# Sigmoid attention and a SwiGLU block on one core: attention in 64x64 tiles of the array, q and k turned by DMA, engine orders written by hand

## The chip, the core and the metric

The kernel runs on one core of one Trainium2 chip. TensorE (PE in the profile, PEld for its weight loads) multiplies, ScalarE (ACT) takes sigmoids, VectorE (DVE) and GpSimd (POOL) copy and cast, and the DMA engines move data; SyncE (SP) and POOL issue the DMAs. The metric is the device time of one run in microseconds (us); lower is better. A program and its data do not change from run to run.

## The reference

```python
B, H, S, D = 8, 12, 448, 64          # q, k, v: float32
scores = q @ k.T / sqrt(D) - log(S)  # for each batch and head
attn   = sigmoid(scores) @ v         # 448 x 64 for each head
x      = attn, heads side by side    # 3584 tokens x 768
g, val = x @ w_gate, x @ w_val       # 768 -> 1536
out    = (g * sigmoid(g) * val) @ w_out   # 1536 -> 768, float32
```

The sigmoid acts on each score by itself, so no sum over a row is needed before the product with v.

## The kernel before, in words

Tokens are cut into chunks of 112 (448 = 4 x 112). For each batch, `emit_load` (L101) brings q, k and v in twelve DMAs of 112 tokens x 12 heads x 64 (pieces of 256 bytes), and `emit_cast` (L109) makes bfloat16 or float16 of them, on GpSimd from the second batch on. `emit_tr` (L121) turns q and k on TensorE, two heads at a time, into tiles of 128 x 448 (rows 0 to 63 hold one head, 64 to 127 the next) through one PSUM buffer, and DVE copies them to SBUF (L132).

For each head, `emit_qk` (L142) makes four score tiles of 112 keys x 448 queries: 64 rows of the array contract, so half of it is used. `emit_sig` takes the sigmoid on ACT (L163). `emit_pv` (L165) multiplies by v: four matmuls with 112 rows and 64 columns. DVE casts the 64 x 448 result into one half of a tile xT (L185), which holds x transposed, 128 features x 448 tokens.

The feed-forward part (FFN) of a batch takes 12 steps f. In each, `emit_ffn1_mm` (L190) runs six matmuls for the gate and six for the value, 128 x 128 weights against 128 x 448 tokens; ACT takes the sigmoid (L205), and DVE makes t (L207) and hT (L209). `emit_ffn2` (L215) makes the output in units of 112 tokens x 384 columns, twelve matmuls each, into the PSUM buffer that the transposes use as well; ACT writes the unit to osb (L230) and POOL issues the store (L235).

A loop over g and j writes attention of batch g, the first FFN part of batch g-1 and the second of batch g-2 into one another, and the framework's scheduler sets the final order of each engine from that. Weights come in 36 DMAs on SP, three for each j, and are cast on ACT and DVE (L88, L90).

PSUM has eight banks: "A" 4 (scores), "P" 1 (pv), "G" 2 (gate, value), "TO" 1:

```python
ps = psum.tile([128, S], BF16, tag="TO", bufs=1, name="ps_tr")
pv = psum.tile([D, S], FP32, tag="P", bufs=1, name="ps_pv")
o = psum.tile([PC, 384], FP32, tag="TO", bufs=1, name="ps_o")
```

Of the kernel before, what the change touches and what calls it, by code (L numbers as in the profile page):

```python
# [12 lines left out]
COPY = mybir.ActivationFunctionType.Copy  # L13
# [5 lines left out]
def kernel(  # L19
# [10 lines left out]
    nc = tc.nc  # L30

# [3 lines left out]
    PC = 112  # L35
    NC_ = S // PC
    NP = H // 2
    NF = DFF // 128
    HSC = 4096.0
# [5 lines left out]
    psum = ctx.enter_context(tc.tile_pool(name="ps", bufs=1, space=bass.MemoryType.PSUM))  # L45
    stg = ctx.enter_context(tc.tile_pool(name="stg", bufs=1))
    one = ctx.enter_context(tc.tile_pool(name="one", bufs=1))
    two = ctx.enter_context(tc.tile_pool(name="two", bufs=2))
    wp = ctx.enter_context(tc.tile_pool(name="wp", bufs=1))
    attn = ctx.enter_context(tc.tile_pool(name="attn", bufs=4))  # L50
    ptp = ctx.enter_context(tc.tile_pool(name="ptp", bufs=8))
    xtp = ctx.enter_context(tc.tile_pool(name="xtp", bufs=12))
    htp = ctx.enter_context(tc.tile_pool(name="htp", bufs=22))
    osp = ctx.enter_context(tc.tile_pool(name="osp", bufs=2))

    idn = one.tile([PC, PC], BF16, tag="idn")
    make_identity(nc, idn)
    sb_t = one.tile([128, 1], FP32, tag="sbiast")
    nc.gpsimd.memset(sb_t, sbias)

    wg16 = [wp.tile([128, DFF], FP16, tag=f"wg{j}", name=f"wg16_{j}") for j in range(NP)]
    wv16 = [wp.tile([128, DFF], FP16, tag=f"wv{j}", name=f"wv16_{j}") for j in range(NP)]
    wo16 = [wp.tile([128, DM], FP16, tag=f"wo{f}", name=f"wo16_{f}") for f in range(NF)]

    wjobs = []
    for j in range(NP):
        rows = slice(j * 128, (j + 1) * 128)
        for h2 in range(2):
            cols = slice(h2 * DM, (h2 + 1) * DM)
            wjobs.append((moe_w_gate[rows, cols], wg16[j][:, cols]))  # L70
            wjobs.append((moe_w_val[rows, cols], wv16[j][:, cols]))
    for f in range(NF):
        rows = slice(f * 128, (f + 1) * 128)
        wjobs.append((moe_w_out[rows, :], wo16[f][:, :]))
    NWJ = len(wjobs)
    wstage = {}

    def emit_wload(i):
        src, _ = wjobs[i]
        st = stg.tile([128, DM], FP32, tag="wst", bufs=4, name=f"wst{i}")  # L80
        nc.sync.dma_start(out=st, in_=src)
        wstage[i] = st

    def emit_wcast(i, eng=None):
        _, dst = wjobs[i]
        eng = eng or nc.scalar
        if eng is nc.scalar:
            eng.copy(out=dst, in_=wstage.pop(i))  # L88
        else:
            eng.tensor_copy(out=dst, in_=wstage.pop(i))  # L90

    q16 = {}
# [24 lines left out]

    qTt = {}
    kTt = {}

    def emit_tr(b, p, which):  # L121
        src = (q16, k16)[which][b]
        ps = psum.tile([128, S], BF16, tag="TO", bufs=1, name="ps_tr")
        for c in range(NC_):
            nc.tensor.transpose(  # L125
                out=ps[:, c * PC:(c + 1) * PC],
                in_=src[:, c, 2 * p:2 * p + 2, :],
                identity=idn,
            )
        d, nm = ((qTt, "qT"), (kTt, "kT"))[which]  # L130
        t = attn.tile([128, S], BF16, tag=nm, name=f"{nm}_{b}_{p}")
        nc.vector.tensor_copy(out=t, in_=ps)  # L132
        d[(b, p)] = t

    def emit_tr_sched(g, j):
        if j < 8:
            btr, ptr = g, j // 2 + 2
        else:
            btr, ptr = g + 1, (j - 8) // 2
        if btr < B and ptr < NP:  # L140
            emit_tr(btr, ptr, j % 2)

    def emit_qk(b, h, cs):
        p, which = divmod(h, 2)
        ro = which * D
        qT = qTt[(b, p)]
        kT = kTt[(b, p)]
        outs = []
        for c in cs:
            sc = psum.tile([PC, S], FP32, tag="A", bufs=4, name="ps_sc")  # L150
            nc.tensor.matmul(  # L151
                out=sc,
                lhsT=kT[ro:ro + D, c * PC:(c + 1) * PC],
                rhs=qT[ro:ro + D, :],
                start=True,
                stop=True,
            )
            pt = ptp.tile([PC, S], FP16, tag="pt", name="pt")
            outs.append((sc, pt))
        return outs  # L160

    def emit_sig(sc, pt):
        nc.scalar.activation(out=pt, in_=sc, func=SIGM, bias=sb_t[:PC], scale=qkscale)  # L163

    def emit_pv(b, h, pts):  # L165
        pv = psum.tile([D, S], FP32, tag="P", bufs=1, name="ps_pv")
        for c in range(NC_):
            nc.tensor.matmul(  # L168
                out=pv,
                lhsT=v16[b][:, c, h, :],  # L170
                rhs=pts[c],
                start=(c == 0),
                stop=(c == NC_ - 1),
            )
        return pv

    xT = {}
    hT = {}

    def emit_pvcast(b, h, pv):  # L180
        p, which = divmod(h, 2)
        ro = which * D
        if which == 0:
            xT[(b, p)] = xtp.tile([128, S], FP16, tag="xT", name=f"xT_{b}_{p}")
        nc.vector.tensor_copy(out=xT[(b, p)][ro:ro + D, :], in_=pv[0:D, :])  # L185

    pvq = []

    def emit_ffn1_mm(b, f, gate):
        ps = psum.tile([128, S], FP32, tag="G", bufs=2,  # L190
                       name="ps_g" if gate else "ps_vl")
        w = wg16 if gate else wv16
        for j in range(NP):
            nc.tensor.matmul(  # L194
                out=ps,
                lhsT=w[j][:, f * 128:(f + 1) * 128],
                rhs=xT[(b, j)],
                start=(j == 0),
                stop=(j == NP - 1),
            )  # L200
        return ps

    def emit_ffn1_post(b, f, gps, vps):
# [6 lines left out]
            out=ht, in0=vps, scalar=HSC, in1=t1, op0=MULT, op1=MULT  # L210
        )
        hT[(b, f)] = ht

    osb_cur = [None]

    def emit_ffn2(b, u):
# [141 lines left out]
```

## Time and profile before

| what | value |
|---|---|
| three runs | 645.62, 647.29, 647.56 us; median 647.29 |
| span of the profiled execution | 646.1 us |
| PE, PEld busy | 610.1 us (94%), 297.3 us (46%) |
| ACT, DVE, POOL busy | 321.8 us (50%), 220.9 us (34%), 85.9 us (13%) |
| moved | 58.71 MB, 91 GB/s over the span |

The page gives no device time for the profiled execution other than its span. The span runs from the first to the last instruction; the runs' times also hold what lies around it. An engine's busy time is the union of its instructions. PE's matmuls overlap in the pipeline, so a row of several matmuls lasts longer than the engine needs before the next may start; starts of rows that follow each other tell the pace.

### The profile page before, as it was taken

The page shows a single profiled execution, that of the slowest core. Times are in us where ns is not written, and L with a number is a line of the kernel's source. Part 1 is how long each engine was busy: PE and PEld are TensorE (multiplying, and loading weights), DVE is VectorE, ACT ScalarE, POOL GpSimd, SP SyncE. Part 2 cuts the span into 40 slices and gives each one's busy share as a digit, 9 for nine tenths or more (in the row PEclk, how much of TensorE's full clock was granted, in tenths as well). Part 3 has the DMA queues.
Part 4 walks back from the last instruction along what each step waited for, and adds up shares of the span by engine and source line. Part 5 has one row for each costly group of instructions (what it writes and reads, how often), then busy time and mean ns, then how long its engine had stood idle before and what let it go on. Part 6 is the DMA issues. An engine that isn't in the chain of part 4 may idle for free.

```text
span 646.1 us, 7821 instructions
## 1 busy us (share of the span) xinstructions
PE 610.1 (94%) x3072; PEld 297.3 (46%) x3072; DVE 220.9 (34%) x402; ACT 321.8 (50%) x576; POOL 85.9 (13%) x123
## 2 busy tenths in 40 slices
PE   0899879999999999999999999999999999999985
PEld 0332323344555455444555455544545454546653
DVE  0232326444333432344333433344333433333310
ACT  4767537655545554455445554555445544542221
POOL 0011110351231102210040102110000000000000
PEclk9999999999999999999999999999999999999999
DMA  9956986995695423704092400010010000000112
GB/s 191 203 144 164 231 243 186 208 208 106 137 218 117 102 50 78 136 23 85 22 173 62 87 23 21 22 30 14 22 43 22 1 23 21 22 22 22 44 43 65
DMA packets 138341, 58.71 MB, mean 91 GB/s; under 512 B 131648, under 2 KB 131648, under 8 KB 138304
## 3 DMA queue, kind: packets, MB, share of 16 engines
q1 hardware_dynamic: 135744, 47.19, 35.3%
q0 software_dynamic: 2560, 11.01, 5.5%
q8 instruction: 24, 0.39, 0.3%
q14 instruction: 13, 0.11, 0.1%
HBM read 47.19 MB, written 11.01 MB: 90 GB/s over the span
## 4 chain that ended last, share of the span: by engine, by line
PE 60%; issue 32%; POOL 2%; ACT 2%; SPq 1%; DMA 1%; DVE 1%; POOLq 0%; ACTq 0%
PE ps_sc L151 12%; PE ps_g L194 12%; PE ps_pv L168 12%; PE ps_vl L194 11%; PE ps_o L223 10%; PE ps_tr L125 4%; SPq L106 1%; POOL out_dram L235 1%; DMA kst<-in_k_dram 1%; ACT pt L163 1%; POOL v L116 0%; DVE xT L185 0%; DVE kT L132 0%; ACT wg L88 0%; ACT L163 0%
## 5 line engine op out<-in xcount | busy, mean ns | idle before, releaser
L163 ACT ACTIVATE pt<-ps_sc,sb_t 112x448 f16<-112x448 f32 x384 | 222.4, 636 | 102.2 <-PE ps_sc L151 93.0
L223 PE MATMUL ps_o<-wo,hT 128*112 128x384 f16 x768 | 135.7, 326 | 4.2 <-ACT osb L230 4.2
L194 PE MATMUL ps_g<-xT,wg 128*128 128x448 f16 x576 | 131.7, 361 | 2.2 <-DVE t L207 1.3
L194 PE MATMUL ps_vl<-xT,wv 128*128 128x448 f16 x576 | 129.3, 359 | 0.3 <-DVE t L207 0.3
L151 PE MATMUL ps_sc<-qT,kT 64*112 64x448 bf16 x384 | 121.9, 409 | 2.9 <-ACT pt L163 2.8
L223 PEld LDWEIGHTS <-hT 128*112 128x112 f16 x768 | 99.8, 130 | 35.4 <-issue 5.6
L168 PE MATMUL ps_pv<-pt,v 112*64 112x448 f16 x384 | 110.2, 390 | 1.6 <-ACT pt L163 1.2
L207 DVE TENSOR_TENSOR t<-ps_g,s 128x448 f16<-128x448 f32 x96 | 60.0, 625 | 149.0 <-ACT s L205 148.8
L205 ACT ACTIVATE s<-ps_g 128x448 f16<-128x448 f32 x96 | 52.2, 544 | 91.1 <-PE ps_g L194 89.5
L230 ACT ACTIVATE osb<-ps_o 112x384 f32<-112x384 f32 x64 | 31.4, 491 | 113.5 <-PE ps_o L223 113.5
L194 PEld LDWEIGHTS <-wg 128*128 128x128 f16 x576 | 50.0, 99 | 72.3 <-issue 35.5
L194 PEld LDWEIGHTS <-wv 128*128 128x128 f16 x576 | 50.0, 98 | 68.2 <-issue 31.2
L185 DVE CAST xT<-ps_pv 64x448 f16<-64x448 f32 x96 | 59.3, 617 | 61.0 <-PE ps_pv L168 60.3
L209 DVE SCALAR_TENSOR_TENSOR hT<-ps_vl,t 128x448 f16<-128x448 f32 x96 | 60.0, 625 | 46.7 <-PE ps_vl L194 44.6
L235 POOL DMA_DIRECT2D out_dram<-osb x32 | 17.0, 531 | 364.6 <-ACT osb L230 364.6
L151 PEld LDWEIGHTS <-kT 64*112 64x112 bf16 x384 | 35.8, 133 | 59.3 <-issue 56.9
L168 PEld LDWEIGHTS <-v 112*64 112x64 f16 x384 | 36.4, 114 | 54.1 <-issue 36.5
L132 DVE COPY qT<-ps_tr 128x448 bf16<-128x448 bf16 x48 | 18.7, 389 | 76.2 <-PE ps_tr L125 76.2
L132 DVE COPY kT<-ps_tr 128x448 bf16<-128x448 bf16 x48 | 18.7, 389 | 64.2 <-PE ps_tr L125 64.2
L125 PE MATMUL ps_tr<-idn,q 112*128 112x112 bf16 x192 | 21.6, 233 | 16.4 <-ACT q L114 14.5
L116 POOL CAST q<-qst 112x768 bf16<-112x768 f32 x28 | 22.6, 830 | 86.6 <-DMA qst<-in_q_dram 62.6
L116 POOL CAST v<-vst 112x768 f16<-112x768 f32 x28 | 22.9, 843 | 79.6 <-DMA vst<-in_v_dram 40.6
(20 smaller groups left out, 107.7 us busy)
## 6 DMA issues: line engine op xcount, KB each, us to landing
qst<-in_q_dram SPq DMA_DIRECT2D x32, 336.0 KB, 5.9
kst<-in_k_dram SPq DMA_DIRECT2D x32, 336.0 KB, 6.2
vst<-in_v_dram SPq DMA_DIRECT2D x32, 336.0 KB, 5.6
out_dram<-osb POOLq DMA_DIRECT2D x32, 336.0 KB, 3.0
wst<-in_moe_w_gate_dram SPq DMA_DIRECT2D x12, 384.0 KB, 4.2
wst<-in_moe_w_val_dram SPq DMA_DIRECT2D x12, 384.0 KB, 4.5
wst<-in_moe_w_out_dram SPq DMA_DIRECT2D x12, 384.0 KB, 3.8
```

The lines of the kernel that those rows point to most:

```text
L116: eng.tensor_copy(out=t[:, c], in_=st)
L125: nc.tensor.transpose(out=ps[:, c * PC:(c + 1) * PC], in_=src[:, c, 2 * p:2 * p + 2, :], identity=idn,)
L132: nc.vector.tensor_copy(out=t, in_=ps)
L151: nc.tensor.matmul(out=sc, lhsT=kT[ro:ro + D, c * PC:(c + 1) * PC], rhs=qT[ro:ro + D, :], start=True, stop=True,)
L163: nc.scalar.activation(out=pt, in_=sc, func=SIGM, bias=sb_t[:PC], scale=qkscale)
L168: nc.tensor.matmul(out=pv, lhsT=v16[b][:, c, h, :], rhs=pts[c], start=(c == 0), stop=(c == NC_ - 1),)
L185: nc.vector.tensor_copy(out=xT[(b, p)][ro:ro + D, :], in_=pv[0:D, :])
L194: nc.tensor.matmul(out=ps, lhsT=w[j][:, f * 128:(f + 1) * 128], rhs=xT[(b, j)], start=(j == 0), stop=(j == NP - 1),)
L205: nc.scalar.activation(out=s16, in_=gps, func=SIGM)
L207: nc.vector.tensor_tensor(out=t1, in0=gps, in1=s16, op=MULT)
L209: nc.vector.scalar_tensor_tensor(out=ht, in0=vps, scalar=HSC, in1=t1, op0=MULT, op1=MULT)
L223: nc.tensor.matmul(out=o, lhsT=hT[(b, f)][:, tci * PC:(tci + 1) * PC], rhs=wo16[f][:, half * 384:(half + 1) * 384], start=(f == 0), stop=( ...
```

## The change

The whole body is written anew. Its parts:

- Four heads make a group; there are 24 groups (three for each batch). Heads 2j and 2j+1 lie on partitions 0 to 63 and heads 6+2j and 7+2j on 64 to 127. Tokens are taken as (p c) with c = 7, so a DMA piece is 1,792 bytes (`load`, two DMAs of 64 partitions for each of q, k and v).
- `cast` makes 128 x 896 tiles. For the first three groups `trans_pe` turns q and k on TensorE (42 matmuls in all); for the other 21 groups `trans_dma` has SP issue a DMA transpose from SBUF to SBUF, 42 in all.
- `qk_tile` makes 64 keys x 448 queries of four heads with four matmuls, each in a quarter of the array of 64 rows x 64 columns; `pv` does the same for the product with v. There are 168 tiles, so 672 matmuls of each kind. One sigmoid covers 128 x 896 elements.
- The FFN's first part stays (1,152 matmuls); the second works on 128 tokens across two batches: 28 chunks x 2 halves x 12 matmuls = 672 of them, evicted on DVE.
- `manual_schedule` leaves each engine's order as the code writes it: FFN units one after another, and between them "visits" of two score tiles of the next batch, with `pv` of a finished group.
- PSUM: two score buffers of two banks, and four banks "G" for all else. Weights come in 18 DMAs of 768 KB through three buffers; gate and value are cast on DVE, w_out on POOL.

Cut to its core:

```diff
-    psum = ctx.enter_context(tc.tile_pool(name="ps", bufs=1, space=bass.MemoryType.PSUM))
+    ctx.enter_context(tc.manual_schedule())
+    psA = ctx.enter_context(tc.tile_pool(name="psA", bufs=2, space=bass.MemoryType.PSUM))
+    psG = ctx.enter_context(tc.tile_pool(name="psG", bufs=4, space=bass.MemoryType.PSUM))
...
+    def load(n, which):
+        b, j = divmod(n, NJ)
+        src = (q, k, v)[which]
+        st = stg.tile([128, 2, S], FP32, tag="stg", name=f"st{which}_{n}")
+        for w in range(2):
+            h0 = w * (H // 2) + 2 * j
+            nc.sync.dma_start(
+                out=st[w * 64:(w + 1) * 64],
+                in_=src[b, h0:h0 + 2].rearrange("h (p c) d -> p h (c d)", c=C),
+            )
...
+    def trans_dma(n, which):
+        t = q16.pop((n, which))
+        d = qkT.tile([128, C, 128], BF16, tag=f"T{which}", name=f"T{which}_{n}")
+        nc.sync.dma_start_transpose(out=d, in_=t.rearrange("p c h d -> p (c h d)"))
+        qT[(n, which)] = d
...
+    def qk_tile(n, c):
+        sc = psA.tile([128, 2, 512], FP32, tag="A", name="ps_sc")
+        qt, kt = qT[(n, 0)], qT[(n, 1)]
+        for w in range(2):
+            for h2 in range(2):
+                r = slice(h2 * 64, h2 * 64 + 64)
+                nc.tensor.matmul(
+                    out=sc[w * 64:(w + 1) * 64, h2, :S],
+                    lhsT=kt[r, c, w * 64:(w + 1) * 64],
+                    rhs=qt[r, :, w * 64:(w + 1) * 64],
+                    start=True,
+                    stop=True,
+                )
+        return sc
+
+    def sig_tile(n, c, sc):
+        pt = ptp.tile([128, 2, S], FP16, tag="pt", name="pt")
+        nc.scalar.activation(out=pt, in_=sc[:, :, :S], func=SIGM, bias=sb_t, scale=qkscale)
+        pts[(n, c)] = pt
+
+    def pv(n):
+        b, j = divmod(n, NJ)
+        P = [psG.tile([128, S], FP32, tag="G", name=f"ps_pv{w}") for w in range(2)]
+        vt = v16.pop(n)
+        for c in range(C):
+            pt = pts.pop((n, c))
+            for h2 in range(2):
+                for w in range(2):
+                    r = slice(w * 64, w * 64 + 64)
+                    nc.tensor.matmul(
+                        out=P[w][h2 * 64:(h2 + 1) * 64, :],
+                        lhsT=vt[r, h2, c * D:(c + 1) * D],
+                        rhs=pt[r, h2, :],
+                        start=(c == 0),
+                        stop=(c == C - 1),
+                    )
+        for w in range(2):
+            x = xtp.tile([128, S], FP16, tag="xT", name=f"xT_{b}_{w * NJ + j}")
+            nc.vector.tensor_copy(out=x, in_=P[w])
...
+    def ffn2(b, m, half):
...
+        o = psG.tile([128, hw], FP32, tag="G", name="ps_o")
+        for f in range(NF):
+            h = hT[(b // 2, f)].rearrange("p b s -> p (b s)")
+            lhsT = h[:, m * 128:(m + 1) * 128]
...
+        nc.vector.tensor_scalar(
+            out=osb[:, half * hw:(half + 1) * hw], in0=o, scalar1=HREC, scalar2=None, op0=MULT
+        )
...
+    for dur, u in units:
+        while vi < len(visits) and tcur >= vtime[vi]:
+            group = visits[vi]
+            vi += 1
+            pvs, pend = pend, []
+            attn_step(group, pvs)
...
+                        if casted <= nn:
+                            cast(nn, 0, nc.gpsimd)
+                            cast(nn, 1, nc.gpsimd)
+                            trans_dma(nn, 0)
+                            trans_dma(nn, 1)
+                            cast(nn, 2, nc.gpsimd)
...
+        while wcq and ui >= 1.5 * wk:
+            kind, i = wcq.pop(0)
+            w_cast(kind, i, nc.gpsimd if kind == "o" else nc.vector)
+            if wl:
+                w_load(*wl.pop(0))
+            wk += 1
```

`attn_step` runs `qk_tile` for the two tiles of a visit, then `pv` of a group that is finished, then the two sigmoids.

The order on ACT in the middle of the run, which follows the matmuls on PE: pt is a score tile's sigmoid, s a gate's, osb an output unit.

```order
L205 ACTIVATE s_1532<-ps_g 128x448
L163 ACTIVATE pt<-ps_sc,sb_t 112x448 x3
L230 ACTIVATE osb_0_1470<-ps_o 112x384
L163 ACTIVATE pt<-ps_sc,sb_t 112x448
L205 ACTIVATE s_1603<-ps_g 128x448
```

```order
L159 ACTIVATE pt<-ps_sc,sb_t 128x896 x2
L199 ACTIVATE s_1414<-ps_g 128x448
L199 ACTIVATE s_1433<-ps_g 128x448
L159 ACTIVATE pt<-ps_sc,sb_t 128x896 x2
L199 ACTIVATE s_1466<-ps_g 128x448
```

The first fence is the kernel before, four narrow sigmoids for each gate with an output unit among them; the second is the change, two wide ones for one or two gates, and the output unit has left ACT.

The order on DVE where the first batch's FFN begins: t and hT free a gate's and a value's PSUM bank, wg and wv are weights, and wst is the buffer that their DMA fills.

```order
L90 CAST wv_4_102<-wst_390 128x768
L90 CAST wv_4_102<-wst_430 128x768
L207 TENSOR_TENSOR t_715<-ps_g,s_713 128x448
L90 CAST wv_5_103<-wst_469 128x768
L207 TENSOR_TENSOR t_769<-ps_g,s_767 128x448
L209 SCALAR_TENSOR_TENSOR hT_0_717<-ps_vl,t_715 128x448
```

```order
L180 CAST xT_5_519<-ps_pv_488 128x448
L201 TENSOR_TENSOR t_577<-ps_g,s_575 128x448
L87 CAST wg_2_105<-wst_g_467 128x1536
L206 SCALAR_TENSOR_TENSOR hT_0_589<-ps_vl,t_577 128x448
L87 CAST wv_2_111<-wst_v_469 128x1536
L201 TENSOR_TENSOR t_617<-ps_g,s_615 128x448
L87 CAST wg_3_106<-wst_g_471 128x1536
L206 SCALAR_TENSOR_TENSOR hT_1_629<-ps_vl,t_617 128x448
```

Before, nearly all value weights are cast ahead of the first t; in the change a third of the gate and value weights are, and the other casts stand between the t and hT of the first FFN steps.

The order on SP in the change at the same place; T_5 are the turned q and k of group 5, c_0 and c_1 their casts on POOL, st the loads.

```order
L81 DMA wst_v_669<-in_moe_w_val_dram 128x6x256
L81 DMA wst_o_692<-in_moe_w_out_dram 128x2x768
L99 DMA st_6_742<-in_q_dram 64x2x448 x2
L99 DMA st_6_745<-in_k_dram 64x2x448 x2
L99 DMA st_6_748<-in_v_dram 64x2x448 x2
L124 DMA_TRANSPOSE T_5_755<-c_0_5_751 128x7x128
L124 DMA_TRANSPOSE T_5_757<-c_1_5_753 128x7x128
L81 DMA wst_o_773<-in_moe_w_out_dram 128x2x768
```

The transposes stand in the same queue as all loads; the rest of w_out comes behind the loads of group 6 and the transposes of group 5.

## Rows read from the trace of the kernel before

**Rows 1.** The page: the span, and part 1, busy time by engine.

```profile
span 646.1 us, 7821 instructions
...
PE 610.1 (94%) x3072; PEld 297.3 (46%) x3072; DVE 220.9 (34%) x402; ACT 321.8 (50%) x576; POOL 85.9 (13%) x123
```

**Rows 2.** Busy time by stage: stretch, length, engines (instructions), granted clock, DMA share, GB/s.

```profile
20.00:60.00 40.00, 37.06 (x115) 12.95 (x114) 11.04 (x22) 28.48 (x49) 5.18 (x6) 1.00 0.65 159
60.00:100.00 40.00, 33.04 (x110) 11.91 (x110) 12.48 (x26) 18.91 (x31) 5.33 (x6) 1.00 0.88 229
...
300.00:400.00 100.00, 100.00 (x533) 50.20 (x532) 35.56 (x65) 50.59 (x95) 15.77 (x22) 1.00 0.29 63
400.00:500.00 100.00, 100.00 (x535) 50.21 (x533) 35.68 (x65) 50.54 (x94) 9.51 (x14) 1.00 0.09 25
```

**Rows 3.** PE in order of time from 303.9 us: start, length, row, count.

```profile
304.00 0.58 PE L151 MATMUL ps_sc<-qT,kT 64*112 64x448 bf16 x2
304.51 1.31 PE L194 MATMUL ps_g<-xT,wg 128*128 128x448 f16 x6
305.75 0.58 PE L151 MATMUL ps_sc<-qT,kT 64*112 64x448 bf16 x2
306.27 1.31 PE L194 MATMUL ps_vl<-xT,wv 128*128 128x448 f16 x6
307.41 2.11 PE L223 MATMUL ps_o<-wo,hT 128*112 128x384 f16 x12
309.46 0.38 PE L168 MATMUL ps_pv<-pt,v 112*64 112x448 f16 x1
```

**Rows 4.** PE in order of time, 18 to 36 us.

```profile
26.78 0.62 PE L151 MATMUL ps_sc<-qT,kT 64*112 64x448 bf16 x1
...
34.32 0.62 PE L151 MATMUL ps_sc<-qT,kT 64*112 64x448 bf16 x2
```

**Rows 5.** Groups by line: count, busy us, mean ns of one, idle before.

```profile
L163 ACT ACTIVATE pt<-ps_sc,sb_t 112x448 f16<-112x448 f32 x384 | 222.4, 636 | 102.2 <-PE ps_sc L151 93.0 <-PE ps_pv L168 8.7
...
L209 DVE SCALAR_TENSOR_TENSOR hT<-ps_vl,t 128x448 f16<-128x448 f32 x96 | 60.0, 625 | 46.7 <-PE ps_vl L194 44.6 <-PE ps_tr L125 0.6
L207 DVE TENSOR_TENSOR t<-ps_g,s 128x448 f16<-128x448 f32 x96 | 60.0, 625 | 149.0 <-ACT s L205 148.8
L185 DVE CAST xT<-ps_pv 64x448 f16<-64x448 f32 x96 | 59.3, 617 | 61.0 <-PE ps_pv L168 60.3
L205 ACT ACTIVATE s<-ps_g 128x448 f16<-128x448 f32 x96 | 52.2, 544 | 91.1 <-PE ps_g L194 89.5 <-PE ps_tr L125 1.6
...
L230 ACT ACTIVATE osb<-ps_o 112x384 f32<-112x384 f32 x64 | 31.4, 491 | 113.5 <-PE ps_o L223 113.5
L116 POOL CAST v<-vst 112x768 f16<-112x768 f32 x28 | 22.9, 843 | 79.6 <-DMA vst<-in_v_dram 40.6 <-issue 39.0
```

**Rows 6.** DMA: queues (packets, MB, share of 16 engines) and issues (us to landing).

```profile
q1 hardware_dynamic: 135744, 47.19, 35.3%
q0 software_dynamic: 2560, 11.01, 5.5%
...
qst<-in_q_dram SPq DMA_DIRECT2D x32, 336.0 KB, 5.9
...
out_dram<-osb POOLq DMA_DIRECT2D x32, 336.0 KB, 3.0
wst<-in_moe_w_gate_dram SPq DMA_DIRECT2D x12, 384.0 KB, 4.2
```

**Rows 7.** The chain of waits from 88 to 100 us: start, length, what.

```profile
94.17 2.40 PE ps_vl L194 x6
...
98.81 1.26 PE ps_vl L194 x6
```

**Rows 8.** All engines in order of time from 638 us; in brackets the idle time before.

```profile
638.10 2.11 PE L223 MATMUL ps_o<-wo,hT 128*112 128x384 f16 x12 [0.63 <-ACT osb L230]
...
641.03 0.53 POOL L235 DMA_DIRECT2D out_dram<-osb  x1 [4.90 <-ACT osb L230]
```

More of the change, by code (lines that the diff above doesn't have):

```diff
@@ new lines, in w_cast @@
+    def w_cast(kind, i, eng):
+        dst = {"g": wg16, "v": wv16, "o": wo16}[kind][i]
+        st = wstage.pop((kind, i))
+        eng.tensor_copy(out=dst.rearrange("p a b -> p (a b)"), in_=st)
+    qkv_st = {}
+    q16, v16, qT = {}, {}, {}
+    def load(n, which):
[8 more added lines that the diff above has]
+            )
+        qkv_st[(n, which)] = st
@@ L87, in emit_wcast, with cast @@
+    def cast(n, which, eng):
+        st = qkv_st.pop((n, which))
+        if which == 2:
+            t = v16p.tile([128, 2, S], FP16, tag="v16", name=f"v16_{n}")
+            v16[n] = t
+            o, i = t, st
+        else:
+            t = c16.tile([128, C, 2, D], BF16, tag="c16", name=f"c16_{which}_{n}")
+            q16[(n, which)] = t
+            o = t.rearrange("p c h d -> p h c d")
+            i = st.rearrange("p h (c d) -> p h c d", c=C)
         if eng is nc.scalar:
-            eng.copy(out=dst, in_=wstage.pop(i))
+            eng.copy(out=o, in_=i)
@@ L135, in emit_tr_sched @@
[L135 to L201, printed above, removed]
@@ new lines, in ffn2 @@
+            for i in range(2):
+                bb, c = divmod(2 * m + i, C)
+                bb += b - b % 2
+                dst = out[bb * S:(bb + 1) * S, :].rearrange("(p c) n -> c p n", c=C)[c]
+                nc.gpsimd.dma_start(out=dst, in_=osb[i * 64:(i + 1) * 64, :])
+    FU1, FU2 = 1.13, 1.93
+    units = []
+    f1_start = {}
+    tt = 0.0
+    for b in range(B):
+        f1_start[b] = tt
+        for f in range(NF):
+            units.append((FU1, ("g", b, f)))
+            units.append((FU1, ("v", b, f)))
+            tt += 2 * FU1
+        for m in range(3) if b % 2 == 0 else range(3, 7):
+            for half in range(2):
+                units.append((FU2, ("o", b, m, half)))
+                tt += FU2
@@ new lines, with attn_step @@
+    tiles = [(n, c) for n in range(NJ, NQ) for c in range(C)]
+    visits = [tiles[i:i + 2] for i in range(0, len(tiles), 2)]
+    LEAD = 6.0
+    vtime = []
+    for grp in visits:
+        n, c = grp[0]
+        b, j = divmod(n, NJ)
+        frac = (j * C + c) / (NJ * C)
+        vtime.append(f1_start[b - 1] + frac * (f1_start[b] - f1_start[b - 1]) - LEAD)
+    def attn_step(group, pvs):
+        scs = [(n, c, qk_tile(n, c)) for n, c in group]
+        for n in pvs:
+            pv(n)
+        for n, c, sc in scs:
+            sig_tile(n, c, sc)
@@ new lines @@
+    for w in (0, 1, 2):
+        load(0, w)
+    for w in (0, 1, 2):
+        load(1, w)
+    cast(0, 0, nc.vector)
+    cast(0, 1, nc.scalar)
+    cast(0, 2, nc.gpsimd)
+    trans_pe(0, 0)
+    trans_pe(0, 1)
+    for w in (0, 1, 2):
+        load(2, w)
+    cast(1, 0, nc.gpsimd)
+    cast(1, 1, nc.vector)
+    cast(1, 2, nc.gpsimd)
+    w_load("g", 0)
+    w_load("v", 0)
+    b0 = [(n, c) for n in range(NJ) for c in range(C)]
+    pend_pv = []
+    wq = [("g", 1), ("v", 1), ("g", 2), ("v", 2), ("g", 3), ("v", 3), ("g", 4), ("v", 4), ("g", 5), ("v", 5)]
```

322 lines of the change are left out of this document (144 added, 178 removed).

## The prediction

> **What bounds the kernel now.** I read the page's busy time first, then the table by stage, then PE in order of time. PE is busy 94% of 646.1 us, no other engine over 50% [rows 1]. By stage, PE is busy for the whole of 300 to 500 us, with ACT and DVE near half and DMA under a third [rows 2]; from 20 to 100 us it is busy 37 and 33 of 40 us, and there the DMA share is 0.65 and 0.88. So there is a long stage in which PE alone counts, and a start that shares the blame with loads. In the long stage PE does (533 + 535) matmuls in 200 us, and a batch has 384 (48 scores, 48 pv, 144 gate and value, 96 output, 48 transposes): 384 / 5.34 = 71.9 us a batch.
>
> What one piece of work takes is read from starts that follow each other [rows 3]. Six value matmuls: 307.41 - 306.27 = 1.14 us, 0.19 each, which is 448 columns at 2.4 GHz. Six gate matmuls followed by scores: 1.24, so a change of the array's form costs 0.10. Twelve output matmuls followed by pv: 2.05, so 1.95 without that change. Two scores: 0.51; less 0.10 and twice 0.19 leaves 0.03 to 0.04, the second's weight load, which is not hidden.
>
> **The parts and their cost.** The span is built anew, since everything moves: a start up to a time T1 at which the first batch's gate and value are done and w_out is loaded, then PE work, then the end.
>
> *FFN.* Gate and value stay: 7 batches after T1, 7 x 24 x 1.14 = 191.5 us. The output part falls from 768 to 672 matmuls, 56 units of 1.95: 109.2 us. Before, a unit at the end waits 0.63 us for the single PSUM buffer [rows 8]; four buffers remove that.
>
> *Scores and pv.* 168 tiles, each with four matmuls for scores and four for pv: 336 packs of four. What one pack takes is the unknown of this change. The trace bounds it on one side: one score matmul alone takes 0.62 us at the low pace, and a row of two takes the same 0.62 us [rows 4]. Heads that are neighbours lie on rows 0 to 63 and 64 to 127, so two different halves of the rows work at once. That two halves of the columns do so too is in no row. If all four quarters run together, a pack takes one stream and one weight load that nothing hides, 0.19 + 0.03 = 0.22; if only the row halves do, twice that, 0.44. I take 0.22: each quarter has its own weights and its own PSUM bank or partitions, as the two row halves have, and the nearest row shows such parts working side by side at no extra time. After T1 there are six batches of 42 packs and 10 packs of the second batch's end: 262 x 0.22 = 57.6 us.
>
> *Changes of form.* About 65 visits after T1, into the quarters and out of them: 65 x 0.20 = 13.0 us. Scores and pv share one visit and one form.
>
> *q and k transposed by DMA.* 384 transposes leave PE, 42 stay, at the start. The 42 DMA transposes of 224 KB have no row. By pieces of one row of 128 bfloat16, 256 bytes, which are the pieces of the q, k and v loads: queue q1 took 35.3% of 16 x 646.1 us for 135,744 packets [rows 6], 27 ns each, so 896 pieces on 16 engines take 1.5 us, and with a landing like a store's 3.0 us it is about 3. If it goes in pieces of 32 bytes instead, 7,168 of them, 12 us. I take 3, since its bytes lie nearest to the 336 and 384 KB transfers, 3.0 to 5.9 us [rows 6]. Cover: a group lasts 52.4 / 3 = 17.5 us (below), its loads 1.38 MB at 260 GB/s 5.3 us, its stores 1.5 us, two transposes 6: 13 us of 17.5. The cover is gone at 5.3 us a transpose. They stand on SP behind two POOL casts (0.843 us for 768 elements [rows 5], so 0.98 for 896), and loads queue behind them; scores of that group come five tiles, some 12 us, later. On POOL those casts queue behind stores that wait for an output unit, 1.95 us at most by the written order, which fits into the 12.
>
> *ACT.* One sigmoid of 448 takes 0.636 us, and from 384 to 448 elements ACT grows by 0.544 - 0.491 = 0.053 [rows 5], 0.83 ns each, so 896 take 0.636 + 0.37 = 1.01. A batch: 21 x 1.01 + 12 x 0.544 = 27.7 us. DVE: 24 x 0.625 + 6 x 0.617 + 7 output units at about that = 23 us. Both hide behind 52 us of PE.
>
> *The start.* Before T1 these must land: groups 0 to 6 (9.6 MB), all weights (14.2 MB) and six transposes (1.4 MB), 25.2 MB, because w_out is queued on SP behind the loads of group 6. The rate: q1, mostly 256-byte pieces, made 47.19 MB in 3,649 us of engine time, 207 GB/s on 16 engines; the store queue with pieces of 3 KB and more made 11.01 MB in 569 us, 310 GB/s; the stretch 60 to 100 us with both kinds 229 at a share of 0.88, so 260 [rows 2, 6]. The change's pieces (1 to 3 KB) lie between; I take 260: 97 us, with POOL's last cast 99, so T1 = 100. Bounds: 310 gives 83, 207 gives 124. PE alone could not be much earlier than 90: until about 35 us it waits for ACT (21 tiles x 1.01 after the first loads), and the first 24 units then run at a low clock, because DVE's weight casts stand between the evictions and wait for loads. Before, six value matmuls take 2.40 us while PE waits often and 1.26 us once work is dense [rows 7], paces of 1.2 and 2.4 GHz, though the table shows a granted clock of 1.00 throughout [rows 2]: 35 + 24 x 2.3 = 90, less what is already fast, plus nine visits.
>
> *The end.* From the last matmul's issue to the span's end: 646.1 - 638.10 - 2.11 = 5.9 us [rows 8], kept.
>
> **Sum**: 100 + 191.5 + 109.2 + 57.6 + 13.0 + 5.9 = 477.2 us of span; 2 for stalls at PSUM, and 1.2 for what lies around the span (the median of the runs is 647.3 against 646.1): **480 us**. A batch in the middle: 24 x 1.14 + 7 x 1.95 + 42 x 0.22 + 10.5 x 0.20 = 52.4 us instead of 71.9.
>
> **Rivals.** *Pairs.* Two score matmuls on the same rows show the second's weight load as 0.03 to 0.04 us that is not hidden [rows 3], while matmuls that use all rows go at 0.19 with theirs. If a weight load must wait until the rows it goes to are free, the third matmul of a pack (rows 0 to 63 again, other columns) cannot start beside the first, and a pack is two pairs: 0.44. Then 262 x 0.44 = 115.3, and the time is 538 us. The rule of the Trainium skill (TensorE: Matmul & The Clock Gate, Part 3, "What overlaps and what doesn't") says this: a weight load overlaps a running matmul only if its row group differs. By that rule this rival is the result; its TensorEngine Tiling (Array Packing), Key Properties, has different tiles load and multiply in parallel, which would give the forecast. The trace agrees with both as far as it goes: it holds no two column halves.
>
> *The transposes bind.* With T for one, a group takes DMA 6.8 + 2T; over 21 groups from 28 us on, and 45 us of PE work behind the last. At T = 5.3 it equals the forecast; it passes 646 us from T = 10.2 on, and at the bound of 12 us it is 28 + 21 x 30.8 + 45 = 720: slower. For it: 32-byte pieces are possible, and no row excludes them. Against: the row of 256-byte loads, and that all DMA after 200 us is far from full before. The Trainium skill (DMA: Bandwidth & Descriptors, "Latency and other measured facts") gives 261 GB/s for DMA transposes, an estimate of 0.9 us for one; the sum would stay at 480.
>
> *A late start.* At 207 GB/s T1 is 124 and the time 504, with PE idle between 40 and 100 us. For it: DVE is held by weight casts, so one late load stops evictions.
>
> **How the numbers follow.** Four abreast 0.55 (462 to 505, from T1 = 90 to 124 and packs of 0.20 to 0.24), pairs 0.28 (515 to 560), transposes as the bound 0.11, of which 0.05 over 646; the rest is late start with something else (0.03) or quicker than 462 (0.03). The range 462 to 560 leaves out some 13 in 100. The three runs spread by 0.3%, about what a measurement of this kernel tells from no change: faster by more 0.94, within it 0.01, slower 0.05.
>
> **What would show it.** Right: score and pv rows in which four matmuls take about 0.22 us from start to start of packs; about 52 us from one batch's first gate to the next; PE without idle time from 100 us on; DMA share near 1 until 95 us; transposes landing in about 3 us. Pairs: packs of 0.44 and 62 us a batch. Transposes: PE idle, ended by the T tiles' DMA, and landings over 5 us. Wrong in kind: a middle stage in which ACT or DVE ends PE's waits, or FFN units that pace at 2.3 us after 100 us.

## The result, and the profile after

The changed kernel takes 471.52 us (median of 5 runs, 471.27 to 475.69) beside 645.62 us for the kernel before (median of 5). The ratio is 0.7316, with a 95% interval of 0.7281 to 0.7351. The prediction, 480 us in a range of 462 to 560, holds it. The profiled execution took 475.69 us, with a span of 473.9.

The page of the changed kernel: the span, busy time by engine (part 1), the costliest groups (part 5) and the DMA transposes (part 6).

```profile
span 473.9 us, 7873 instructions
...
PE 428.5 (90%) x3210; PEld 212.9 (45%) x3210; DVE 194.8 (41%) x317; ACT 211.2 (45%) x267; POOL 100.1 (21%) x137
...
L159 ACT ACTIVATE pt<-ps_sc,sb_t 128x896 f16<-128x896 f32 x168 | 159.2, 1005 | 107.4 <-PE ps_sc L148 107.4
...
L148 PE MATMUL ps_sc<-T,T 64*64 64x448 bf16 x672 | 54.2, 388 | 23.1 <-DMA T<-c 15.2
...
L171 PE MATMUL ps_pv<-pt,v 64*64 64x448 f16 x672 | 39.4, 374 | 0.0
...
T<-c SPq DMA_TRANSPOSE x42, 5.5
```

PE is still the engine that counts: 428.5 us busy, where it was 610.1 [rows 1]. The mean of one score or pv matmul, 388 and 374 ns, says little, since four of them run at once; 672 at 388 ns would be 261 us, and the group's busy time is 54.2. PE waits 23.1 us ahead of scores, 15.2 of it for the transposed tiles (T).

The table by stage: stretch, length, PE, PEld, DVE, ACT, POOL (instructions), granted clock, DMA share, GB/s.

```profile
0.00:41.00 41.00, 23.63 (x222) 11.64 (x223) 12.65 (x19) 24.81 (x27) 8.19 (x15) 0.88 1.03 241
41.00:61.00 20.00, 7.09 (x46) 3.14 (x45) 5.63 (x8) 6.03 (x8) 5.60 (x6) 0.77 1.13 245
61.00:93.00 32.00, 29.69 (x214) 13.82 (x215) 17.50 (x27) 15.09 (x20) 5.87 (x4) 0.93 1.06 305
93.00:117.00 24.00, 18.72 (x130) 9.03 (x128) 5.27 (x10) 5.71 (x6) 10.40 (x12) 0.86 0.97 209
200.00:300.00 100.00, 100.00 (x781) 49.66 (x780) 43.07 (x72) 51.39 (x65) 23.36 (x32) 1.00 0.67 139
300.00:400.00 100.00, 100.00 (x757) 49.51 (x758) 43.32 (x72) 50.03 (x64) 20.74 (x29) 1.00 0.47 93
```

There are two stages, as before [rows 2]. In the start DMA is full until about 117 us and PE works 7.09 us of the 20 after 41 us. From 200 to 400 us PE never pauses, DVE and ACT are near half and DMA under 70%. In 100 us PE now does 757 to 781 matmuls instead of 533 to 535.

PE of the changed kernel in order of time: the start, a piece of the middle, the first gate of the last batch, and the last matmuls.

```profile
61.21 0.59 PE L148 MATMUL ps_sc<-T,T 64*64 64x448 bf16 x4 [13.08 <-DMA T<-c]
...
67.11 0.57 PE L148 MATMUL ps_sc<-T,T 64*64 64x448 bf16 x8
67.51 1.49 PE L171 MATMUL ps_pv<-pt,v 64*64 64x448 f16 x28
68.94 1.31 PE L194 MATMUL ps_g<-xT,wg 128*128 128x448 f16 x6
...
93.03 1.46 PE L221 MATMUL ps_o<-wo,hT 128*128 128x384 f16 x8
96.21 0.48 PE L221 MATMUL ps_o<-wo,hT 128*128 128x384 f16 x2 [1.72 <-POOL wo L87]
100.25 0.80 PE L221 MATMUL ps_o<-wo,hT 128*128 128x384 f16 x2 [3.56 <-POOL wo L87]
100.98 0.96 PE L148 MATMUL ps_sc<-T,T 64*64 64x448 bf16 x8
101.87 4.02 PE L221 MATMUL ps_o<-wo,hT 128*128 128x384 f16 x12
105.83 0.89 PE L148 MATMUL ps_sc<-T,T 64*64 64x448 bf16 x8
...
116.39 1.30 PE L194 MATMUL ps_g<-xT,wg 128*128 128x448 f16 x6
...
250.77 1.31 PE L194 MATMUL ps_g<-xT,wg 128*128 128x448 f16 x6
251.92 1.30 PE L194 MATMUL ps_vl<-xT,wv 128*128 128x448 f16 x6
253.05 2.11 PE L221 MATMUL ps_o<-wo,hT 128*128 128x384 f16 x12
255.10 0.57 PE L148 MATMUL ps_sc<-T,T 64*64 64x448 bf16 x8
255.60 4.07 PE L221 MATMUL ps_o<-wo,hT 128*128 128x384 f16 x24
...
423.35 1.30 PE L194 MATMUL ps_g<-xT,wg 128*128 128x448 f16 x6
...
459.69 6.66 PE L221 MATMUL ps_o<-wo,hT 128*128 128x384 f16 x40
```

Again starts tell the pace. Twenty-eight pv matmuls, seven packs: 68.94 - 67.51 = 1.43 us. An output unit ahead of scores lasts 255.10 - 253.05 = 2.05, which is 1.95 and a change of form, 0.10. Without that change the seven packs take 1.33, **0.19 us each**: one stream of 448 columns, and nothing beside it. Two score packs ahead of pv, which has the same form: 67.51 - 67.11 = 0.40, so 0.02 to 0.03 once a visit.

PE of the kernel before, at the first gates of its second and last batches:

```profile
143.91 1.31 PE L194 MATMUL ps_g<-xT,wg 128*128 128x448 f16 x6
...
574.95 0.73 PE L194 MATMUL ps_g<-xT,wg 128*128 128x448 f16 x3
```

With these marks the 172.2 us between the two spans divide without a rest. Up to the second batch's first gate: 143.9 before, 116.4 after, 27.5 us gained. Six batches: (575.0 - 143.9) / 6 = 71.8 before, (423.4 - 116.4) / 6 = 51.2 after, 124.1 gained. From the last batch's first gate to the end: 71.1 before, 50.5 after, 20.6 gained. So seven parts in ten of the gain are the steady stage.

The chain of waits of the changed kernel from 43 us on: start, length, what.

```profile
43.28 4.37 SPq L99
47.70 7.76 DMA st<-in_q_dram
55.46 5.71 DMA T<-c
61.21 0.59 PE ps_sc L148 x4
...
82.81 8.61 DMA wst_o<-in_moe_w_out_dram
91.47 1.47 POOL wo L87
```

Both long waits of the start end with transfers. SP is held 4.37 us issuing a load, the load takes 7.76 and the transpose behind it 5.71; PE stands still for 13.08. The second is w_out: its load, then its cast on POOL. The last two of its six loads are issued at 89.1 and 91.0 us, when casts on POOL (done at 89.03 and 90.99) have freed two of the three weight buffers; the last one lands at 98.0 and is cast from 98.74 on.

### The profile page after: what moved, and what is told of

The parts are those of the page before. It is cut to its first block, busy times and chain, and to the rows that moved or that the text cites. A ratio compares the mean times of both kernels' runs of the same rounds, so it can differ in the third digit from the quotient of the medians.

```text
span 473.9 us, 7873 instructions
## 1 busy us (share of the span) xinstructions
PE 428.5 (90%) x3210; PEld 212.9 (45%) x3210; DVE 194.8 (41%) x317; ACT 211.2 (45%) x267; POOL 100.1 (21%) x137
## 4 chain that ended last, share of the span: by engine, by line
PE 81%; DMA 9%; SPq 5%; POOL 2%; issue 1%; DVE 0%; POOLq 0%; ACT 0%; DVEq 0%
PE ps_o L221 24%; PE ps_vl L194 22%; PE ps_g L194 22%; PE ps_sc L148 7%; PE ps_pv L171 6%; SPq L99 4%; DMA st<-in_k_dram 2%; DMA wst_o<-in_moe_w_out_dram 2%; DMA st<-in_q_dram 2%; DMA st<-in_v_dram 2%; DMA T<-c 1%; POOL wo L87 1%; SPq L124 1%; SPq L81 1%; POOL c L119 1%
## 5 line engine op out<-in xcount | busy, mean ns | idle before, releaser
L159 ACT ACTIVATE pt<-ps_sc,sb_t 128x896 f16<-128x896 f32 x168 | 159.2, 1005 | 107.4 <-PE ps_sc L148 107.4
L221 PE MATMUL ps_o<-wo,hT 128*128 128x384 f16 x672 | 117.2, 330 | 5.3 <-POOL wo L87 5.3
L221 PEld LDWEIGHTS <-hT 128*128 128x128 f16 x672 | 64.3, 99 | 56.5 <-issue 16.5
L148 PE MATMUL ps_sc<-T,T 64*64 64x448 bf16 x672 | 54.2, 388 | 23.1 <-DMA T<-c 15.2
L228 DVE TENSOR_SCALAR osb<-ps_o 128x384 f32<-128x384 f32 x56 | 31.2, 557 | 91.3 <-PE ps_o L221 91.3
L119 POOL CAST c<-st 128x896 bf16<-128x896 f32 x44 | 40.2, 936 | 37.6 <-DMA st<-in_q_dram 26.0
L180 DVE CAST xT<-ps_pv 128x448 f16<-128x448 f32 x48 | 27.7, 619 | 32.4 <-PE ps_pv L171 32.4
L171 PE MATMUL ps_pv<-pt,v 64*64 64x448 f16 x672 | 39.4, 374 | 0.0
L171 PEld LDWEIGHTS <-v 64*64 64x64 f16 x672 | 21.5, 115 | 13.6 <-issue 1.5
L119 POOL CAST v<-st 128x896 f16<-128x896 f32 x24 | 22.4, 933 | 19.7 <-DMA st<-in_v_dram 18.7
```

What stands on the lines that cost most here:

```text
L119: eng.tensor_copy(out=o, in_=i)
L148: nc.tensor.matmul(out=sc[w * 64:(w + 1) * 64, h2, :S], lhsT=kt[r, c, w * 64:(w + 1) * 64], rhs=qt[r, :, w * 64:(w + 1) * 64], start=True, ...
L159: nc.scalar.activation(out=pt, in_=sc[:, :, :S], func=SIGM, bias=sb_t, scale=qkscale)
L171: nc.tensor.matmul(out=P[w][h2 * 64:(h2 + 1) * 64, :], lhsT=vt[r, h2, c * D:(c + 1) * D], rhs=pt[r, h2, :], start=(c == 0), stop=(c == C - 1),
L180: nc.vector.tensor_copy(out=x, in_=P[w])
L221: nc.tensor.matmul(out=o, lhsT=lhsT, rhs=wo16[f // 2][:, f % 2, half * hw:(half + 1) * hw], start=(f == 0), stop=(f == NF - 1),)
```

## The experiments

**Column halves of one row half side by side.** The order of the four matmuls in a pack is turned, for scores and for pv.

```diff
-        for w in range(2):
-            for h2 in range(2):
+        for h2 in range(2):
+            for w in range(2):
                 r = slice(h2 * 64, h2 * 64 + 64)
...
-            for h2 in range(2):
-                for w in range(2):
+            for w in range(2):
+                for h2 in range(2):
                     r = slice(w * 64, w * 64 + 64)
...
```

> The four matmuls of a pack are issued with the two column halves of one row half next to each other, instead of the two row halves. Theory (a quarter waits only for its own rows and columns): a pack stays at 0.21 us from start to start, the time within 0.5% of 471.5 us. Rival (a weight load waits until its rows are free, and the order in the changed kernel hides that by taking turns between the row halves): the second matmul waits for the first, a pack takes 0.40 us or more, and 336 packs make the run 60 us longer, about 530 us.

Measured: 471.66 us (470.99 to 472.55), ratio 0.7326 (0.727 to 0.7383). Nothing changes. Its PE in order of time, beside 255.10 and 255.60 above:

```profile
255.23 0.57 PE L148 MATMUL ps_sc<-T,T 64*64 64x448 bf16 x8
255.73 0.99 PE L221 MATMUL ps_o<-wo,hT 128*128 128x384 f16 x5
```

The visit starts 0.50 us before the next unit in both orders, and the 28 pv matmuls from 82.73 us on take 1.43 us here too. Quarters that share rows did not wait for each other, in either order.

**The pv product, one quarter after the other.**

```diff
-        for c in range(C):
-            pt = pts.pop((n, c))
-            for h2 in range(2):
-                for w in range(2):
+        for h2 in range(2):
+            for w in range(2):
+                for c in range(C):
+                    pt = pts[(n, c)]
...
```

> The product with v is issued quarter by quarter: all seven chunks of one quarter, then the next quarter, so that neighbours in the order use the same quarter. Same matmuls, same results. Theory (matmuls start in order, and side by side only where neighbours use different quarters): a group's 28 matmuls take 28 x 0.19 to 0.21 = 5.3 to 6.0 us instead of 1.32, 4.0 to 4.7 us more; some 22 groups of it on the path make 560 to 575 us. This prices the packing of pv alone. Rival (the engine starts a later matmul whose quarter is free ahead of one that waits, or the gain came from elsewhere): a group stays under 3 us and the time under 510 us.

Measured: 505.21 us (504.74 to 507.23), ratio 0.7857 (0.7783 to 0.793). PE of this kernel in order of time:

```profile
258.41 0.57 PE L148 MATMUL ps_sc<-T,T 64*64 64x448 bf16 x8
258.81 3.28 PE L171 MATMUL ps_pv<-pt,v 64*64 64x448 f16 x28
262.02 1.31 PE L196 MATMUL ps_g<-xT,wg 128*128 128x448 f16 x6
```

The 28 matmuls take 262.02 - 258.81 = 3.21 us, not 1.43. The 1.78 us more, in the 21 groups after the first batch, make 37 us; 33.7 were measured. So the order within pv is worth about 34 us. But 3.21 is also much less than my theory's price. If matmuls started strictly in the order written, only the last of one quarter could run beside the first of the next: 28 less 3 steps of 0.19, 4.75 us.

The starts of single matmuls in the trace show what happens instead. They come 0.189 us apart, the first at 258.81. Right beside the fourth (0.006 us behind it, at 259.383) a second row of seven starts, a third at 259.980 and a fourth at 260.578. The first matmul of each new row lasts 0.373 us, the others 0.349. The trace does not name the quarter, but seven in a row fit one quarter each: the next quarter starts while three matmuls of the one before it are still to come. That is 3 x 3 + 7 = 16 steps of 0.19, 3.04, and with the change of form 3.13, near the 3.21. So PE started matmuls of a later quarter ahead of earlier ones that waited for a busy one, as the rival had it, though a group took more than its 3 us. My theory of the order fell, and only the sign of the cost held.

**All transposes on TensorE.** No DMA transpose is left; each group is turned at the sixth tile of the group before it.

```diff
-                            trans_dma(nn, 0)
-                            trans_dma(nn, 1)
...
+                if c == 5 and n + 1 < NQ:
+                    trans_pe(n + 1, 0)
+                    trans_pe(n + 1, 1)
```

> All q and k are turned on TensorE, seven matmuls and one DVE copy for each tile, placed at the visit with the sixth tile of the group before; no DMA transposes. Theory: 42 tiles x 7 x 0.055 to 0.11 us = 16 to 32 us more on PE, less what the start gives back, where 1.4 MB of transposes at 260 GB/s stand before w_out (5 us) and PE waits 13.1 us for a DMA-made tile: 476 to 492 us. Rival (the DMA transposes cost the start nothing but their bytes): 485 to 500 us. Rival (the DMA transposes slow the loads and so cost more than they save): under 471 us.

Measured: 480.05 us (479.37 to 481.28), ratio 0.7458 (0.74 to 0.7516). PE in order of time, at the start and at the second and last batches' first gates:

```profile
60.64 1.51 PE L171 MATMUL ps_pv<-pt,v 64*64 64x448 f16 x27 [1.99 <-DVE hT L206]
...
107.77 1.30 PE L194 MATMUL ps_g<-xT,wg 128*128 128x448 f16 x6
...
428.02 1.30 PE L194 MATMUL ps_g<-xT,wg 128*128 128x448 f16 x6
```

The wait of 13 us is gone and the second batch starts at 107.8. But a batch takes (428.0 - 107.8) / 6 = 53.4 us instead of 51.2: the transposes by DMA give 13 us in six batches and take some 4 to 9 back in the start (the second batch begins at 112.02 in the kernel with the turned order and at 116.39 in the profiled execution of the change).

**Visits of one score tile.**

```diff
-    visits = [tiles[i:i + 2] for i in range(0, len(tiles), 2)]
+    visits = [tiles[i:i + 1] for i in range(0, len(tiles), 1)]
```

> A visit brings one score tile instead of two: 147 visits instead of 74, nothing else. Theory: each further visit costs two changes of the array's form, 2 x 0.094 us, less nothing: 73 x 0.19 = 13.7 us, about 485 us. Rival (a change of form is hidden where the next weights are loaded meanwhile, or one-tile visits relieve ACT and PSUM): under 475 us.

Measured: 483.79 us (481.82 to 486.04), ratio 0.7515 (0.7452 to 0.7577): 12.3 us more for 73 visits more, 0.17 each. From the second batch's first gate (113.37) to the last batch's (433.71) a batch takes 53.4 us instead of 51.2, 2.2 for 10.5 visits more, 0.21 each; in the start, where PE waits for other things, the visits cost less. The price of a change of form in the sum, 0.20 in and out, is about right.

**One w_out load instead of six.** This one prices the bytes of the start.

```diff
-        st = wstage.pop((kind, i))
+        st = wstage[("o", 0)] if kind == "o" else wstage.pop((kind, i))
...
-    wl = [("v", 3), ("g", 4), ("v", 4), ("g", 5), ("v", 5)] + [("o", i) for i in range(6)]
+    wl = [("v", 3), ("g", 4), ("v", 4), ("g", 5), ("v", 5), ("o", 0)]
```

> Only the first 768 KB of w_out are loaded, and all six parts of w_out are cast from them; five loads, 3.9 MB, are left out. Theory (bytes before w_out set the end of the start: PE has done the first batch's gate and value at 93.0 us and then waits 5.3 us for w_out's casts and runs at the low pace after it): the output units begin at 93 us without waiting, first gate of the second batch at 107 to 110 us instead of 116.4, time 462 to 466 us. Rival (the start ends by PE's own work or by the casts on POOL): under 2 us of gain.

Measured: 465.23 us (464.01 to 465.65), ratio 0.7201 (0.7167 to 0.7235). PE in order of time:

```profile
58.55 0.59 PE L148 MATMUL ps_sc<-T,T 64*64 64x448 bf16 x4 [10.16 <-DMA T<-c]
...
89.86 2.11 PE L221 MATMUL ps_o<-wo,hT 128*128 128x384 f16 x12
...
104.71 1.30 PE L194 MATMUL ps_g<-xT,wg 128*128 128x448 f16 x6
```

No unit waits for w_out, and the first takes 2.04 us (the next row starts at 91.90); 6.3 us are gained, and the second batch begins at 104.71, sooner than the 107 to 110 I expected. The wait for group 4's transposes, 10.16 us, is not touched, since the loads ahead of it stand before w_out. The gain is less than the bytes: 3.9 MB are 13 to 16 us at 240 to 300 GB/s. The first output unit begins only 3 us sooner than the 93.03 of the change, so what comes before it is set by that wait and by PE's own work.

**w_out and the first output units later.** All of the first two batches' output comes behind the second batch's gate and value, and w_out with it.

```diff
-        for m in range(3) if b % 2 == 0 else range(3, 7):
+        for m in range(0) if b == 0 else range(7) if b == 1 else range(3) if b % 2 == 0 else range(3, 7):
...
-        while wcq and ui >= 1.5 * wk:
+        while wcq and ui >= (1.5 * wk if wk < 8 else 24 + 2.0 * (wk - 8)):
...
-            if wl:
+            if wl and (wl[0][0] != "o" or wk >= 8):
...
```

> The first batch's output units move behind the second batch's gate and value, and w_out's loads with them; nothing is left out. Theory (in the start DMA is full, and w_out is what PE waits for at 93 to 101 us): PE goes on with the second batch's gate and value, which need no w_out, at 90 to 100 us; the 8 us of waiting and some 5 us of low pace go: 456 to 463 us. Rival (the loads of q, k and v, moved forward by the denser visits, take the same time, so that PE waits as long elsewhere): within 1% of 471.5 us.

Measured: 473.68 us (472.56 to 474.34), ratio 0.7331 (0.729 to 0.7372). My theory fell here: no unit waits for w_out now, but PE waits as long for other things. The DMA share is 1.13 from 40 to 60 us, 0.98 to 80 and 1.12 to 104. PE still loses 12.95 us at 60.53 to a transposed tile, 2.55 at 79.72 to the next and 0.85 at 87.19 to DVE; all its waits from 40 us on make 19.1 us, beside 17.7 in the kernel with the turned order. In SP's order the loads of the next groups took w_out's place: those of groups 6 and 7 are issued before its first load, and those of group 8 before its last four.

**Weight casts on POOL instead of DVE** (gate and value, in the main loop).

```diff
-            w_cast(kind, i, nc.gpsimd if kind == "o" else nc.vector)
+            w_cast(kind, i, nc.gpsimd)
```

> The gate and value weights of the main loop are cast on POOL instead of DVE, so that no load holds up the evictions on DVE. Theory (DMA bytes bind the start): no gain, since POOL now waits for weights ahead of the casts of q, k and v: 471 to 480 us. Rival (DVE, held by weight casts, stops PE in the start): 460 to 468 us.

Measured: 472.16 us (470.4 to 472.32), ratio 0.7305 (0.7269 to 0.734). No gain, as expected. DVE held by weight casts, which my rival of a late start named, does not set the time.

**Casts and transposes ahead of the loads in each visit.**

```diff
-                        if nn + 1 < NQ and loaded <= nn + 1:
-                            for w in (0, 1, 2):
-                                load(nn + 1, w)
-                            loaded = nn + 2
                         if casted <= nn:
...
+                        if nn + 1 < NQ and loaded <= nn + 1:
+                            for w in (0, 1, 2):
+                                load(nn + 1, w)
+                            loaded = nn + 2
```

> In each visit that loads a group, the casts and DMA transposes of the next group go ahead of the loads of the one after, on SP and POOL. In the changed kernel PE waits 13.1 us at 48 us for transposes that stand on SP behind six loads. Theory (the bytes until w_out set the end of the start, and those stay): that wait shrinks to under 8 us, but the first output unit still begins at 92 to 95 us and waits for w_out: within 0.7% of 471.5 us. Rival (the order on SP sets it): the gain is kept to the end, 460 to 466 us. Rival (SP, held by the transposes' wait for casts, lets the DMA engines run dry): over 476 us.

Measured: 472.32 us (470.89 to 473.12), ratio 0.7311 (0.7275 to 0.7346). The one wait of 13.08 us becomes 4.60 at 53.17, for T, and 3.90 at 62.99, for DVE. The first output unit begins at 87.93, sooner than the 92 to 95 I expected, and still waits for w_out, 2.03 us at 92.51 and 3.57 at 96.56. The queue's order moves the waits and does not shorten the run. POOL ahead of the last wait:

```profile
92.40 1.82 POOL L119 CAST c<-st 128x896 bf16<-128x896 f32 x2
...
95.04 1.47 POOL L87 CAST wo<-wst_o 128x1536 f16<-128x1536 f32 x1
```

The last part of w_out landed at 92.8 us and was cast at 95.04, behind three casts of q, k and v, while the DMA share from 90 to 94 us was 0.45. So this last wait is POOL's order as well as bytes; no run changed that order.

**Attention of two batches first.** The feed-forward part starts when two batches of xT are ready, and uses each part of the weights for both, so that more PE work stands behind each byte. The loads and casts of the start are placed anew for it.

```diff
+    for f in range(NF):
+        for b in range(2):
+            units.append((FU1, ("g", b, f)))
+            units.append((FU1, ("v", b, f)))
...
-    tiles = [(n, c) for n in range(NJ, NQ) for c in range(C)]
+    tiles = [(n, c) for n in range(2 * NJ, NQ) for c in range(C)]
...
```

> Attention of the first two batches stands at the start, and each part of the gate and value weights is then used for both batches before the next part is needed; the first seven output chunks follow. Nothing is left out. Theory (in the start the DMA engines are full and PE lacks work for the bytes that have landed): 42 sigmoids of 1.0 us end at about 55 us, and from there PE has 54.7 us of gate and value work for 9.4 MB of weights that need 36 us, so it no longer waits; all work in the middle is 51.2 us a batch, so 55 + 409 - 17 (attention of two batches done) + 8 at the end = 455 us, 450 to 460. Rival (bytes still bind, w_out and the loads of the third batch with them): within 1% of 471.5 us.

Measured: 478.23 us (477.5 to 479.41), ratio 0.7422 (0.7387 to 0.7457), slower than the change. The table by stage of this kernel:

```profile
40.00:60.00 20.00, 10.14 (x104) 4.89 (x98) 4.65 (x6) 11.77 (x13) 5.68 (x6) 0.59 1.13 249
60.00:80.00 20.00, 18.05 (x146) 9.12 (x147) 10.03 (x15) 12.28 (x15) 2.61 (x2) 0.75 0.93 246
80.00:100.00 20.00, 13.12 (x67) 5.59 (x65) 8.54 (x13) 4.02 (x7) 1.08 (x2) 0.83 1.11 285
```

DMA is at 0.93 to 1.13 all the time, now for q, k and v. The feed-forward part began at 70.7 us instead of the 55 I had set, and a weight then held PE for 6.88 us at 92.58 (DVE, which PE waits for, stood 9.64 us for a load of w_val). Together with the three runs before it, this fits a start that is set mostly by its bytes: in the change 24.5 MB have moved by 93 us, at 241 to 305 GB/s, and no order that I tried shortened the run. That bytes alone set it is not shown: leaving out 3.9 MB gave less than half of their time on the wire, and in the kernel with casts first DMA was half idle when PE's last wait began.

**Three PSUM banks instead of four for all that is not scores.**

```diff
-    psG = ctx.enter_context(tc.tile_pool(name="psG", bufs=4, space=bass.MemoryType.PSUM))
+    psG = ctx.enter_context(tc.tile_pool(name="psG", bufs=3, space=bass.MemoryType.PSUM))
```

> Three PSUM banks instead of four for gate, value, pv and output; nothing else. Theory (with four banks PE never waits for one in the middle of the run, and an eviction takes 0.6 us of DVE or 1.2 us of ACT and DVE together against a unit's 1.14 us): three banks are short only where pv takes two of them, once for each of 21 groups, some 1 us each: 485 to 500 us. Rival (banks do not matter, the gain came from the packing alone): within 0.7% of 471.5 us.

Measured: 471.11 us (470.08 to 472.36), ratio 0.7307 (0.726 to 0.7355). My theory fell, three are as good as four. PE is busy for all of 200 to 300 us here too.

No version with the whole work beat the change by more than its own runs differ. Not tried: the old output units of 112 tokens in the new kernel; packs of two instead of four; the framework's own order of the engines; more than three weight buffers. So the 20.6 us that a batch lost are divided by counting and not by a run. The output part is 1.95 us (one unit of eight less); the other 18.7 are attention with its transposes and changes of form. Within the new kernel, runs price two things: the order inside pv at 3 x 1.78 = 5.3 us a batch, and the transposes by DMA at 2.2.

## Why the prediction was right, point by point

**Four abreast** held, and with it the forecast. A pack takes 0.19 us, not 0.22: the term of the sum, 57.6 us, put a weight load that nothing hides on each of 262 packs, and only the first pack after a change of form shows one, 0.03 on 65 visits. So 262 x 0.19 + 65 x 0.03 = 51.7. I took the load from two score matmuls of one row [rows 3], where both come right behind a change of form; the row could not tell the first load from any.

**Pairs** fell. A pack would have taken 0.44, and it takes 0.19 in either order of its matmuls; its four matmuls start within 0.01 us of each other (255.096 to 255.106 in the change). The Trainium skill's rule (TensorE: Matmul & The Clock Gate, Part 3, "What overlaps and what doesn't"), that a weight load runs beside a matmul only on another row group, does not agree with these runs; what its TensorEngine Tiling (Array Packing), Key Properties, says of tiles that load and multiply in parallel does.

**A batch** was set at 52.4 us and takes 51.2. Gate and value units (251.92 - 250.77 = 1.15) and output units (1.95) are as priced, so 24 x 1.14 + 7 x 1.95 = 41.0 leave 10.2 for attention, where the forecast had 42 x 0.22 + 2.1 = 11.3. ACT's sigmoid of 896, set at 1.01, takes 1.005.

**The start** was set at T1 = 100, and the last two w_out matmuls of the first unit could start at 100.25. The rate was right: 241, 245 and 305 GB/s in the three stages up to 93 us, 264 on average, where I took 260; whether the size of the pieces is the reason, no run tells. That the time came out so close is partly luck, since PE's way there was another one. I had its first 24 units at 2.3 us each from 35 us on, which is 90. They began at 41.36, nearly all took their 1.14, and two waits for T, 13.08 and 2.09 us, made up the rest, so that PE stood at the first output unit at 93.03. The profiled execution has the longer start of those seen: in the kernel with the turned order, which does the same work, w_out is ready at 97.17 and the second batch begins at 112.02 instead of 116.39. That is about the 4 us by which the profiled execution stands above the median.

**The transposes** were set at 3 us and land in 5.5 (median; 5.0 from 200 to 420 us). That is past the 5.3 at which I had the cover gone, and yet PE never pauses from 120 to 440 us. (The formula beside it, 28 + 21 x (6.8 + 2T) + 45, reaches the forecast at T = 6.3; 5.3 is where the sum of one group, 6.8 + 2T, fills its 17.5 us.) The step that failed is that sum: it counts a transpose's landing as time in which all engines work for it. The queue of all loads and transposes, in the change and then in the kernel with all transposes on TensorE (packets, MB, share of 16 engines):

```profile
q1 hardware_dynamic: 70752, 56.84, 56.6%
q1 hardware_dynamic: 31776, 47.20, 39.7%
```

The 42 transposes are the difference: 928 packets each, the 896 pieces that I had counted at 256 bytes and a few more, and 0.566 x 473.9 - 0.397 x 478.6 = 78 us of all engines, 1.9 each, if the loads take the same time in both. So pieces of 256 bytes were right, and those of 32 were not; the engines work 1.9 us for a transpose where I had estimated 1.5, and the rest of the 5.5 is no work of theirs. A group then takes 6.8 + 2 x 1.9 = 10.6 us of DMA, in line with the share of 0.67 from 200 to 300 us. In the start, where the wire is full, the landing and SP's time to issue do show, as the 13.08 us.

**PSUM and the end.** I put 2 us on stalls that did not occur, and three banks show that there was a bank to spare. The end takes 473.9 - (459.69 + 6.66) = 7.5 us from the last matmul to the last store, where I had carried over 5.9 [rows 8].

The sum against the profiled span: 477.2 + 2 forecast, 473.9 measured. The packs give -5.9, the stalls -2.0; the end adds 1.6, and the unit at 101.87, which takes 3.96 us behind a wait instead of 1.95, adds 2.0. Together -4.3 of the -5.3; the last 1.0 I have not traced.

## What to carry to other kernels

A product that contracts and makes only 64 is worth laying out so that four of them fill the array: here a pack of four cost one stream, 0.19 us, in either order tried inside the pack, but the order must go round the quarters (28 matmuls took 1.43 us so, and 3.21 one quarter after the other). A visit to another form cost about 0.2 us, so collect tiles for it. In a start with DMA full, moving work or loads about changed which wait was seen and not the time; leaving bytes out did shorten it, by less than half of their time on the wire. And the time from a transfer's issue to its landing is not the time that it takes from the engines: 5.5 us against 1.9 here.

## What the runs showed of the hardware that I had not expected

- PE did not start matmuls strictly in the order written: 28 of them, seven in each quarter in turn, took 3.21 us where that order allows 4.75 at best, and the next quarter began beside the fourth of seven. The Trainium skill (TensorE: Matmul & The Clock Gate, Part 3, "What overlaps and what doesn't") has matmuls start in program order; that run does not agree.
- The weight load of 64 columns is hidden even behind the matmul of its own quarter (seven in a row 0.189 us apart), and shows only at the first matmul of a quarter, whose next one starts 0.213 us later.
- Behind the waits of 1.72 and 3.56 us at 96.21 and 100.25, twelve output matmuls took 105.83 - 101.87 = 3.96 us, the pace of 1.2 GHz, with a granted clock of 0.50 from 102 to 106 us; behind the 13.08 us wait six value matmuls took 2.22 us (61.73 to 63.95). In the kernel with pv by quarter there is one wait there, of 1.90 us, and the next unit took 100.11 - 98.06 = 2.05, the pace of 2.4 GHz, with a granted clock of 1.00 from 93 to 117 us:

```profile
97.14 0.48 PE L223 MATMUL ps_o<-wo,hT 128*128 128x384 f16 x2 [1.90 <-POOL wo L87]
...
98.06 2.12 PE L223 MATMUL ps_o<-wo,hT 128*128 128x384 f16 x12
100.11 0.38 PE L148 MATMUL ps_sc<-T,T 64*64 64x448 bf16 x4
```
